# A gated block with segmented attention on one core: the issuing engine of small copies, the place of the late modulation vectors, and the order of the first down-weight scaling

## The chip, the cores and the metric

The kernel runs on one core of one Trainium2 chip. The metric is the device time of one execution in microseconds (us); less is better. The median of three runs before the change is 1928.77 us (1926.87 to 1936.36).

## The reference

x has 2048 rows of 576. From a condition c come six vectors of 576: shift, scale and gate for each of two halves (sa, ca, ga, sb, cb, gb).

```
mod = silu(c) @ w_mod                        # 6 vectors of 576
h   = layernorm(x) * (1 + ca) + sa
x   = x + ga * attention(h)                  # 32 heads of 18, 4 segments of 512 rows
h   = layernorm(x) * (1 + cb) + sb
x   = x + gb * ((silu(h @ w_gate) * (h @ w_up)) @ w_down)   # inner width 4608
```

In the attention each segment s of 512 rows has causal softmax attention within itself, mixed by a sigmoid gate per head with a read from a memory: phi(q) M / phi(q) z, where M and z sum phi(k) v and phi(k) over the earlier segments and phi(t) is t + 1 for t > 0 and exp(t) otherwise. Everything is in float32.

## The kernel before, in words

Products of two float32 matrices are made from a rounded high part and a remainder (hi and lo), so one product is three matmuls. The program has three stages.

**Stage 1, projections (up to about 261 us in the trace).** A loop goes over the four segments s. Within a segment, nine column groups t of q and k are projected (`proj`, matmuls in `mm14` at L99), then four row groups of v (`vproj`, L481 copies the result out). At the end of a segment come the memory sums (`mem`, L433 and L436) and the transposed, scaled input of the next segment (`trans_in`: transposes at L232, ScalarE at L239, and a split into hh on GpSimd, L79, and hl on VectorE, L80). In this stage a scheduler orders each engine's instructions, so that the order on an engine isn't that of the source. Beside the projections run generators, which the loop advances by `next` some times per column or row group:

- `prep(s + 1)` loads and normalises the next segment's rows;
- `late_mod()`, only in segment 1, makes the four vectors that are needed later (p = 2, 4, 3, 5, that is ga, cb, sb, gb). Each is a sum over six blocks k of 96 rows of w_mod: the block is loaded into wml (two buffers) by SyncE, L377, and VectorE multiplies it by one column of silu(c) and adds it to macc (`mod_mul`, L292 for the first and L294 for the others; macc has one buffer). Then TensorE sums macc over its 96 partitions: as a row for all partitions for ga and gb (`mod_row`, L313 into pc, copied to gaB or gbB by ScalarE at L314), as columns for cb and sb (`mod_col`, L301 and L304, L307 and L308). Before the last row group of v, the loop runs out whatever is left of the generators;
- `early()`, from segment 1 on, computes the row maxima of the first attention units.

**Stage 2, attention (about 261 to 656 us).** From here on the order of instructions is written out by hand (`tc.manual_schedule()`). The work is cut into 32 units u of four heads and one segment. A unit has two passes. The first (`p1_step`, matmul L182, VectorE L187) finds each row's maximum of the scores; it is done one or two units ahead. The second (`p2_step`, L579) computes the scores again with the maximum taken off in the same matmul: the stationary kst and the moving qst have 108 rows of data, and rows 108 and 109 of qst hold the negated maxima (hi and lo). ScalarE takes the exponential straight out of PSUM (L582, two PSUM banks s2), GpSimd masks, and TensorE multiplies by v (`av_step`, L599). Between the passes, the maxima of unit u + 1 are transposed (`mt_a`, L201, event m), copied out of PSUM to mr by ScalarE and written into rows 108 and 109 of its qst by two small DMAs (`mt_b`, L205, and `put_m`, L170, event n). One DMA of `put_m` is 16 x 128 numbers, 8 KB. `PAT` is a table that says after which of a unit's eleven steps an event's instructions are issued; event n stands at step 4 of most units, at step 2 of the odd ones in the second half of a segment. SyncE issues nearly all other DMAs of the stage, in program order: the four of `load_stack` for unit u + 3 (L164 and L165), vq, qf (L752), woraw (L884), xr (L676), and stores of xD, xh and yD. An engine that issues a DMA waits in its own order for what the DMA needs.

**Stage 3, feed-forward (about 656 us to the end).** Two halves of the rows t, and in each 18 periods p of two inner blocks, each with 14 steps k of seven matmuls of 512 columns (`prod`, L1180); the down products (L1284, L1301) are worked in a period later. Gate and up weights arrive as O (`load_o`, L1113, two buffers), GpSimd forms four sums of them (`sum_o`, L1135), ScalarE and VectorE split them into wh and wl (`prep_w`, L1144 and L1145). For t = 0 the two rows of blocks of w_down are loaded (`load_d`, L1152), scaled by gbB on GpSimd (`mul_d`, L1158), combined by four differences (`sum_d`, L1163), split for use (`prep_d`, L1169 and L1170), and the whole is stored for t = 1 (L1494). In the first period (`dl` = 2) the steps of `mul_d`, `sum_d` and `prep_d` come two later than in the others: products at steps 6 and 7, differences at 8 to 11, splits at 8 to 11.

The lines of the loop body that set this:

```
if k == 1:
    load_d(0, p)
elif k - dl in (4, 5):
    mul_d(p, k - 4 - dl)
if tn == 0 and 4 <= k < 8:
    sum_o(nx, 0, k - 4)
...
if k - dl in (6, 7, 8, 9) and p < NPR - 2:
    sum_d(p, k - 6 - dl)
```

Of the kernel before, what the change touches and what calls it, by code (L numbers as in the profile page):

```python
# [7 lines left out]
F32 = mybir.dt.float32  # L8
# [9 lines left out]
D = 576  # L18
# [49 lines left out]
def f32(ap):  # L68
    return ap.bitcast(F32)
# [3 lines left out]
def block(ctx: ExitStack, tc: tile.TileContext, x, wqk, wv, wo, beta, wgu, wd, c, w_mod, out):  # L73
    nc = tc.nc
    def pool(stk, name, bufs=1, **kw):
        return stk.enter_context(tc.tile_pool(name=name, bufs=bufs, reuse_waits="tile", **kw))
# [9 lines left out]
    def run(g):  # L86
        for _ in g:
            pass
# [29 lines left out]
    qst, kst = {}, {}  # L118
# [39 lines left out]
    def load_stack(u, b):  # L158
        s, q = units[u]
        for e in range(2):  # L160
            v = [d[s].rearrange("f z t -> (f z) t").rearrange("(Q a e r) t -> Q e r a t", Q=8, a=2, e=2)[q, e]
                 for d in (kD, qD)]
            r = slice(54 * e, 54 * e + 54)
            nc.sync.dma_start(f32(kst[b][r]), v[0])  # L164
            nc.sync.dma_start(f32(qst[b][r, e:4:2, :]), v[1])  # L165

    def put_m(u, b):
        mr = mrow.pop(u)
        for a in range(2):
            nc.scalar.dma_start(f32(qst[b][108 + a:109 + a]).rearrange("p a t -> p (a t)"), mr[16 * a:16 * a + 16])  # L170

    def p1_step(u, b, i, ps, jp, jb):
        if i == 3:
# [34 lines left out]
    def p1_unit(u, b, ps, tag, bufs, jp, jb):  # L208
        for i in range(4):
            yield from p1_step(u, b, 3 - i, ps, jp, jb)  # L210
        mt_a(u, ps, tag, bufs)
        mt_b(u)
# [29 lines left out]
    with ExitStack() as p1:  # L242
        wq1 = pool(p1, "wq1")
        raw = pool(p1, "raw1", 2)
# [6 lines left out]
        def early():  # L251
            for u in range(2):
                load_stack(u, u)
            for u in range(NE):
                yield from p1_unit(u, u, ps, "m", 1, pb, 2)
            load_stack(2, 2)
# [26 lines left out]
        wmv = w_mod.rearrange("(k p) (s f) -> s p k f", p=96, s=6)  # L283
# [6 lines left out]
        def mod_mul(a, t, k):  # L290
            if k == 0:
                nc.vector.tensor_scalar(a, t, sg[:, 0:1], None, op0=ALU.mult)  # L292
            else:
                nc.vector.scalar_tensor_tensor(a, t, sg[:, k:k + 1], a, op0=ALU.mult, op1=ALU.add)  # L294
# [22 lines left out]
        with ExitStack() as p0:  # L317
# [41 lines left out]
            for b in range(3):  # L359
                n = P if b < 2 else 64  # L360
# [8 lines left out]
        pk = pb.tile([P, 4, 640], F32, tag="pk", name="pk", bufs=1)  # L369
        nc.gpsimd.memset(pk[:, :, 0:64], 0.0)  # L370

        def late_mod():
            for p in (2, 4, 3, 5):
                a = raw.tile([96, D], F32, tag="macc", name="macc", bufs=1)
                for k in range(6):
                    t = raw.tile([96, D], F32, tag="wml", name="wml", bufs=2)
                    nc.sync.dma_start(t, wmv[p][:, k, :])  # L377
                    mod_mul(a, t, k)
                    if k % 2:
                        yield  # L380
                if p == 2:
                    mod_row(a, gaB)
                elif p == 4:
                    mod_col(a, 0, 1.0)
                elif p == 3:
                    mod_col(a, 1, 0.0)
                else:
                    mod_row(a, gbB)
                yield

        hT = {}

        def trans_in(s):
            hh = [h1.tile([P, L], F32R, tag=f"hh{k}", name=f"hh{k}") for k in range(4)]
            hl = [h1.tile([P, L], F32R, tag=f"hl{k}", name=f"hl{k}") for k in range(4)]
            hr = h1.tile([P, L], F32R, tag="hr", name="hr")
            hT[s] = (hh, hl, hr)
            for kt in range(5):
                pt = ps.tile([P, L], F32, tag="t", name="pt")
                transpose_group(pt, lambda i: xs[s][:, i, :], kt)  # L400
                if kt < 4:
                    evac_split(wk, pt, kt, hh[kt], hl[kt], colv[:, kt, 0:1], colv[:, kt, 1:2])
                else:
                    evac_split(wk, pt, kt, hr, None, colv[:, kt, 0:1], colv[:, kt, 1:2])
                yield
# [92 lines left out]
        for s in range(NSEG):  # L498
            gens = []
            if s == 0:  # L500
                gens.append(load_wv())
            if s + 1 < NSEG:
                gens.append(prep(s + 1))
            if s == 1:
                gens.append(late_mod())
            g = chain(*gens)
            if s == 1:
                for b in range(3):
                    new_stack(b, sk)
                ge = early()  # L510
            pend = None
            for t in QKORD:
                if s == 0 and t + 4 < 9:
                    load_qk(t + 4)
                f = proj(s, t)
                if pend is not None:
                    phi_k(s, *pend)
                    pend = None
                if t < 5 and s < 3:
                    pend = (t, f)  # L520
                if s > 0 or t > 1:
                    next(g, None)
                    next(g, None)
                if s > 0:
                    for _ in range(E1):
                        next(ge, None)
            tg = trans_in(s + 1) if s + 1 < NSEG else iter(())
            for i in range(4):
                if i == 3:
                    for _ in g:  # L530
                        pass
                vproj(s, i)
                next(g, None)
                next(g, None)
                if s > 0:
                    for _ in range(E2):
                        next(ge, None)
                if i == 2:
                    next(tg, None)
            next(tg, None)  # L540
            if s < 3:
                for _ in mem(s):
                    next(tg, None)
            for _ in tg:
                pass
        run(ge)

    p2, p2r = ExitStack(), ExitStack()
    sk2 = pool(p2, "sk2")
# [345 lines left out]
    NPR = NF // 2  # L895
# [260 lines left out]
    def mul_d(p, f):  # L1156
        v = RW[p][:, 2 * f:2 * f + 2].rearrange("p a b -> p (a b)")
        nc.gpsimd.tensor_tensor(v, v, gbB, op=ALU.mult)  # L1158

    def sum_d(p, j):  # L1160
        r = RW[p]
        d, a, b = ((4, 1, 0), (5, 3, 4), (6, 2, 5), (1, 3, 1))[j]
        nc.gpsimd.tensor_tensor(r[:, d], r[:, a], r[:, b], op=ALU.subtract)  # L1163
# [156 lines left out]
    with tc.manual_schedule():  # L1320
# [5 lines left out]
        for u in range(NU + 1):  # L1326
            s, q = divmod(u, 8)
# [48 lines left out]
        for i in range(4):  # L1376
            for h in range(2):
                for c in range(WC):
                    n = 8 * i + 4 * h + c
# [4 lines left out]
                    if n in SS:  # L1384
                        j = SS.index(n)
# [3 lines left out]
                    if n in WW:  # L1389
                        j = WW.index(n)  # L1390
# [20 lines left out]
        n, nw = 0, PF  # L1411
# [5 lines left out]
        for t in range(2):  # L1417
            for p in range(NPR):
                last = t == 1 and p == NPR - 1
                dl = 2 if t == 0 and p == 0 else 0  # L1420
# [14 lines left out]
                for k in range(14):  # L1435
# [23 lines left out]
                    if t:  # L1459
                        if k == 2 + swap:  # L1460
                            prep_r(1, p, 1)
                        elif not last and k == 9:
                            prep_r(1, nx, 0)
                    else:
                        if k in (3, 5):
                            prep_r(0, p, 1, k // 5)
                        elif tn == 0 and k in (9, 10):
                            prep_r(0, nx, 0, k - 9)
                        elif tn and k == 8:
                            prep_r(1, 0, 0)  # L1470
                        if k == 1:
                            load_d(0, p)
                        elif k - dl in (4, 5):
                            mul_d(p, k - 4 - dl)
                        if tn == 0 and 4 <= k < 8:
                            sum_o(nx, 0, k - 4)
                        elif tn == 0 and k in (10, 11):
                            sum_o(nx, 1, 2 * k - 20)
                            sum_o(nx, 1, 2 * k - 19)
                        if k - dl in (6, 7, 8, 9) and p < NPR - 2:  # L1480
                            sum_d(p, k - 6 - dl)
                        if k == 0 and p == 0:
                            store_o(p, 0)
                            store_o(p, 1)
                        elif k == 3:
                            store_r(p, 0)
                        elif k == 8:
                            store_r(p, 1)
                        elif k == 11 and tn == 0:
                            store_o(nx, 0)  # L1490
                        elif k == 13 and tn == 0:
                            store_o(nx, 1)
                        if k == 12 + dl // 2:
                            nc.scalar.dma_start(wdD[p][:, :NS[p]], RW[p][:, :NS[p]])  # L1494
# [28 lines left out]
                    if is_plain(t, p):  # L1523
                        if k in DK[dl // 2]:
                            j = DK[dl // 2].index(k)
# [74 lines left out]
```

## Time and profile before

| | |
|---|---|
| Median of three runs | 1928.77 us |
| Profiled execution, its own time | 1926.03 us |
| Span of that execution, first to last instruction | 1924.3 us |
| Granted TensorE clock over the span, mean | 0.996 |
| DMA moved | 301.82 MB, 157 GB/s |
| SyncE's hardware queue (q1) | 242.27 MB |
| ScalarE's hardware queue (q10) | 57.60 MB |

Times in the profile are microseconds from the first instruction, unless ns is given. Engines are PE (TensorE matmuls), PEld (its weight loads), DVE (VectorE), ACT (ScalarE), POOL (GpSimd), SP (SyncE); a q behind the name is the engine's sequencer, which issues DMAs. L12 is line 12 of the kernel. In a row of the time order stand the start, the duration, the engine, the line, the operation and tiles (out <- in), how many were merged, and in brackets how long the engine was idle before and what ended that. A row of waits reads: who waited, for whom, us in total, times, longest. A row of the chain of waits has start, duration and name; the chain is followed back from the last instruction, at each step to what released it. A row of a group ends with busy time, mean ns of one, and the idle time before them.

### The profile page before, as it was taken

How to read it: one execution, taken by the hardware profiler on the slowest of the kernel's cores; microseconds unless marked ns; L12 is line 12 of the kernel's file. 1: busy time of each engine (PE TensorE's matmuls, PEld its weight loads, DVE VectorE, ACT ScalarE, POOL GpSimd, SP SyncE). 2: the span in 40 equal slices, each digit the busy share in tenths (PEclk: the TensorE clock that was granted, in tenths of full speed). 3: DMA queues.
4: the chain of work that ended last, by engine and by line, in shares of the span. 5: the costliest groups of instructions: out<-in, count | busy, mean ns of one | idle time of the engine just before them, and what ended most of it. 6: DMA issues, size and time to landing. Idle time of an engine off the chain costs nothing.

```text
span 1924.3 us, 30666 instructions
## 1 busy us (share of the span) xinstructions
PE 1879.5 (98%) x10927; PEld 1561.4 (81%) x10927; DVE 1505.2 (78%) x3270; ACT 930.7 (48%) x2057; POOL 584.3 (30%) x787
## 2 busy tenths in 40 slices
PE   7999999999999999999999999999999999999999
PEld 4887865676666778888888888888888888888888
DVE  6575258777786688898897988876888888888887
ACT  1222257767767544445445445444544444454542
POOL 5212235455546453545444544410000000000000
PEclk9999999999999999999999999999999999999999
DMA  6776465455743855454454554478333233333331
GB/s 197 259 244 218 166 210 138 121 151 144 195 137 112 274 185 184 150 187 158 160 182 153 168 169 144 138 244 269 101 111 108 80 122 101 122 101 96 105 108 61
DMA packets 177856, 301.82 MB, mean 157 GB/s; under 512 B 26024, under 2 KB 106344, under 8 KB 175912
## 3 DMA queue, kind: packets, MB, share of 16 engines
q1 hardware_dynamic: 147080, 242.27, 40.7%
q10 hardware_dynamic: 30624, 57.60, 8.5%
q8 instruction: 86, 1.41, 0.3%
q14 instruction: 66, 0.54, 0.1%
HBM read 186.73 MB, written 112.53 MB: 156 GB/s over the span
## 4 chain that ended last, share of the span: by engine, by line
PE 89%; DVE 3%; DMA 3%; ACT 2%; issue 1%; ACTq 1%; POOL 1%; SPq 0%; DVEq 0%; POOLq 0%
PE A L1180 23%; PE pd L1301 13%; PE C L1180 12%; PE pd L1284 9%; PE B L1180 6%; PE pp L99 5%; PE s L579 4%; PE av L599 3%; PE s L182 3%; PE pv L99 3%; PE pw L709 2%; ACT Pt L582 1%; ACTq L170 1%; PE pn L780 1%; PE pm L433 1%
## 5 line engine op out<-in xcount | busy, mean ns | idle before, releaser
L1180 PE MATMUL A<-y,wh 128*128 128x512 f32 x1152 | 406.6, 393 | 1.9 <-ACT tc L1209 1.0
L187 DVE CUSTOM_DVE_ANT_0 junk<-s,tri 128x256 bf16<-128x256 f32 (+3 forms) x512 | 229.1, 487 | 78.8 <-PE s L182 71.3
L1145 DVE TENSOR_TENSOR wl<-O,wh 128x256 fp32r<-128x256 f32 x504 | 259.4, 520 | 2.5 <-ACT wh L1144 2.0
L1180 PEld LDWEIGHTS A<-y,wh 128*128 128x128 f32 x1152 | 217.0, 188 | 46.5 <-ACT tc L1209 1.8
L582 ACT ACTIVATE Pt<-s 128x512 f32<-128x512 f32 (+1 forms) x352 | 185.5, 559 | 88.0 <-PE s L579 49.5
L1180 PE MATMUL A<-y,wl 128*128 128x512 f32 x576 | 227.0, 394 | 0.0
L1135 POOL TENSOR_TENSOR O<-O 128x384 f32<-128x384 f32 x144 | 163.8, 1149 | 180.5 <-DMA O<-in_wgu_dram 85.8
L1289 DVE TENSOR_TENSOR acc<-acc,pd 128x576 f32<-128x576 f32 x216 | 162.5, 752 | 58.7 <-PE pd L1284 51.5
L1180 PE MATMUL C<-y,wh 128*128 128x512 f32 x576 | 203.1, 393 | 3.8 <-DVE cu L1203 3.8
L1144 ACT CAST wh<-O 128x256 fp32r<-128x256 f32 x504 | 196.8, 405 | 0.8 <-issue 0.8
L1301 PE MATMUL pd<-dh,ah 128*128 128x288 f32 x640 | 189.1, 295 | 0.0
L1301 PE MATMUL pd<-dh,al 128*128 128x288 f32 x640 | 189.1, 295 | 0.0
L1301 PE MATMUL pd<-dl,ah 128*128 128x288 f32 x640 | 188.9, 295 | 0.0
L1305 DVE TENSOR_TENSOR acc<-acc,pd 128x576 f32<-128x576 f32 x156 | 116.9, 750 | 85.3 <-PE pd L1301 84.7
L579 PE MATMUL s<-qs,ks 110*128 110x512 f32 (+2 forms) x384 | 151.7, 411 | 10.9 <-ACT Pt L582 8.9
L1244 ACT CAST ah<-sg 128x512 fp32r<-128x512 f32 x192 | 119.1, 621 | 84.6 <-DVE sg L1204 84.4
L1245 DVE TENSOR_TENSOR al<-sg,ah 128x512 fp32r<-128x512 f32 x192 | 137.1, 714 | 10.8 <-ACT ah L1244 10.6
L182 PE MATMUL s<-ks,qs 108*128 108x256 f32 (+3 forms) x512 | 140.1, 326 | 1.4 <-DVE mx L187 1.4
L1284 PE MATMUL pd<-dh,ah 128*128 128x288 f32 x448 | 133.0, 297 | 0.0
L1284 PE MATMUL pd<-dh,al 128*128 128x288 f32 x448 | 132.5, 296 | 0.0
L1284 PE MATMUL pd<-dl,ah 128*128 128x288 f32 x448 | 132.3, 295 | 0.0
L1180 PEld LDWEIGHTS C<-y,wh 128*128 128x128 f32 x576 | 108.4, 188 | 24.5 <-DVE cu L1203 4.2
(357 smaller groups left out, 4407.8 us busy)
## 6 DMA issues: line engine op xcount, KB each, us to landing
O<-in_wgu_dram SPq DMA_DIRECT2D x36, 768.0 KB
oD<-O ACTq DMA_DIRECT2D x36, 512.0 KB
O<-oD SPq DMA_DIRECT2D x36, 512.0 KB
ks<-kD SPq DMA_DIRECT2D x64, 216.0 KB
qs<-qD SPq DMA_DIRECT2D x64, 216.0 KB
O<-in_wgu_dram SPq DMA_DIRECT2D x36, 384.0 KB
rD<-wr ACTq DMA_DIRECT2D x36, 336.0 KB
wr<-rD SPq DMA_DIRECT2D x35, 336.0 KB
```

Source lines behind the costliest of these rows:

```text
L99: nc.tensor.matmul(ps, lhsT=a, rhs=b, start=(k == 0), stop=(k == 13))
L182: nc.tensor.matmul(bank[:, n * (h - h0):n * (h - h0) + n], lhsT=qst[b][0:108, h, 128 * i:128 * i + 128], rhs=kst[b][0:108, h // 2, 0:n], s ...
L187: nc.vector.tensor_tensor_reduce(junk[:, :n], bank[:, n * (h - h0):n * (h - h0) + n], tri[:, L - n:], 1.0, -3e38, op0=ALU.add, op1=ALU.max ...
L579: nc.tensor.matmul(bank[:, n * (g - h):n * (g - h + w)].rearrange("p (a b) -> p a b", a=w), lhsT=kst[u % NB][0:110, g // 2, 128 * j:128 * ...
L582: nc.scalar.activation(pt[:, h:h + per, :n], bank[:, :n * per].rearrange("p (a b) -> p a b", a=per), AF.Exp, scale=SCALE)
L1135: nc.gpsimd.tensor_tensor(o[:, d], o[:, a], o[:, b], op=op)
L1144: nc.scalar.copy(wh, o)
L1145: later.append(lambda: nc.vector.tensor_tensor(wl, o, f32(wh), op=ALU.subtract))
L1180: nc.tensor.matmul(bank, lhsT=a, rhs=b, start=(first and n == 0), stop=(n == 6), skip_group_check=not first)
L1284: nc.tensor.matmul(pd[:, i, :288], lhsT=a[:, tk], rhs=w, start=(k == 0), stop=(k == 2))
L1289: nc.vector.tensor_tensor(o, o, pd[:, :, :288], op=ALU.add)
L1301: nc.tensor.matmul(pd[:, i, :288], lhsT=a[:, tk], rhs=w, start=(k == 0), stop=(k == 5))
```

## The change

Three edits stand in one diff.

- **A.** The two DMAs of `put_m` are issued by SyncE in place of ScalarE: 64 in all, 60 of them in stage 2.
- **B.** `late_mod` leaves the chain of generators of segment 1. It becomes a generator of its own, made in segment 1 and advanced once after each of the last three row groups of v there, and once after each column and row group in segments 2 and 3. It yields once per block and once more per vector. A block's load is issued one step ahead of its `mod_mul`.
- **C.** In the first feed-forward period only, the down weights are loaded in step 0 (before: step 1), both products and the first three differences are issued in step 2 (before: steps 6, 7, 8, 9 and 10), the fourth in step 11 as before. Thereby they stand ahead of the `sum_o` instructions of steps 4 to 7 in GpSimd's order.

In the instruction order that comes out, SyncE's DMAs from stage 2 on are those of before with the 60 copies put in: in a unit they stand behind the loads of unit u + 3 and ahead of the qf, woraw or xr loads. The instruction order on GpSimd in the first period is two products, three differences, four sums of O, two sums, the fourth difference, two sums. On VectorE, the four accumulations that finish ga stand between the hl instructions ahead of segment 2, and the six of sb among those ahead of segment 3; the pc matmuls of gb come behind the last matmul of segment 3.

```diff
     def put_m(u, b):
         mr = mrow.pop(u)
         for a in range(2):
-            nc.scalar.dma_start(f32(qst[b][108 + a:109 + a]).rearrange("p a t -> p (a t)"), mr[16 * a:16 * a + 16])
+            nc.sync.dma_start(f32(qst[b][108 + a:109 + a]).rearrange("p a t -> p (a t)"), mr[16 * a:16 * a + 16])
...
+        def load_ml(p, k):
+            t = raw.tile([96, D], F32, tag="wml", name="wml", bufs=2)
+            nc.sync.dma_start(t, wmv[p][:, k, :])
+            return t
+
         def late_mod():
-            for p in (2, 4, 3, 5):
-                a = raw.tile([96, D], F32, tag="macc", name="macc", bufs=1)
-                for k in range(6):
-                    t = raw.tile([96, D], F32, tag="wml", name="wml", bufs=2)
-                    nc.sync.dma_start(t, wmv[p][:, k, :])
-                    mod_mul(a, t, k)
-                    if k % 2:
-                        yield
+            pk_ = [(p, k) for p in (2, 4, 3, 5) for k in range(6)]
+            t = load_ml(*pk_[0])
+            for n, (p, k) in enumerate(pk_):
+                nt = load_ml(*pk_[n + 1]) if n < 23 else None
+                yield
+                if k == 0:
+                    a = raw.tile([96, D], F32, tag="macc", name="macc", bufs=1)
+                mod_mul(a, t, k)
+                t = nt
+                if k < 5:
+                    continue
+                yield
                 if p == 2:
                     mod_row(a, gaB)
...
                     mod_row(a, gbB)
-                yield
...
-            if s == 1:
-                gens.append(late_mod())
             g = chain(*gens)
             if s == 1:
...
                 ge = early()
+                gl = late_mod()
...
+                if s > 1:
+                    next(gl, None)
...
                     for _ in range(E2):
                         next(ge, None)
+                    if s > 1 or i > 0:
+                        next(gl, None)
...
         run(ge)
+        run(gl)
...
-                        if k == 1:
+                        if k == 1 - dl // 2:
                             load_d(0, p)
-                        elif k - dl in (4, 5):
-                            mul_d(p, k - 4 - dl)
+                        elif dl and k == 2:
+                            mul_d(p, 0)
+                            mul_d(p, 1)
+                            for j in range(3):
+                                sum_d(p, j)
+                        elif dl and k == 11:
+                            sum_d(p, 3)
+                        elif not dl and k in (4, 5):
+                            mul_d(p, k - 4)
...
-                        if k - dl in (6, 7, 8, 9) and p < NPR - 2:
-                            sum_d(p, k - 6 - dl)
+                        if not dl and k in (6, 7, 8, 9) and p < NPR - 2:
+                            sum_d(p, k - 6)
```

## The prediction, made before the changed kernel was run

> **What bounds the kernel now.** I read the page first, then the busy time by stage.
>
> ```profile
> span 1924.3 us, 30666 instructions
> PE 1879.5 (98%) x10927; PEld 1561.4 (81%) x10927; DVE 1505.2 (78%) x3270; ACT 930.7 (48%) x2057; POOL 584.3 (30%) x787
> ```
>
> TensorE is busy 98% of the span and no other engine is near it, so an edit can pay only where TensorE stands still or runs at a lower clock. The stretches of the three edits show how much of that there is. The columns are: length, busy time and instructions of each engine, granted clock, DMA share, GB/s.
>
> ```profile
> 96.00:131.00 35.00, 34.03 (x181) 27.48 (x180) 31.90 (x91) 7.35 (x15) 7.12 (x11) 1.00 0.77 246
> 148.00:160.00 12.00, 7.82 (x27) 5.18 (x26) 5.16 (x7) 2.19 (x5) 2.35 (x3) 0.72 0.43 163
> 170.00:219.00 49.00, 48.78 (x294) 42.91 (x293) 17.79 (x32) 13.91 (x25) 11.16 (x18) 1.00 0.49 180
> 208.00:220.00 12.00, 11.54 (x77) 9.86 (x76) 5.13 (x10) 3.39 (x5) 4.66 (x9) 1.00 0.26 108
> 261.00:640.00 379.00, 366.05 (x2646) 244.31 (x2645) 289.44 (x1179) 269.07 (x556) 204.51 (x387) 1.00 0.53 147
> 656.00:692.00 36.00, 30.28 (x120) 23.07 (x119) 29.71 (x46) 21.34 (x48) 16.41 (x14) 0.95 0.74 249
> 730.00:1924.00 1194.00, 1190.03 (x6512) 1046.94 (x6510) 1002.01 (x1673) 554.85 (x1285) 259.93 (x234) 1.00 0.44 140
> ```
>
> After 730 us there is nothing to win (4.0 us idle in 1194), and none of the edits acts there. What can be won lies in three places: the end of segment 1 (148 to 160: 4.2 us idle and a clock of 0.72), the attention stage (261 to 640: 13.0 us idle), and the first feed-forward period (656 to 692: 5.7 us idle and a clock of 0.95).
>
> **Edit B, modulation vectors over two segments.** The waits of TensorE from 131 to 170 us, then of VectorE from 96 to 170, then the group of the accumulations, then rows of TensorE and ScalarE in order of time, and one of the chain:
>
> ```profile
> PE pc L313 <- DVE macc L294: 2.5, 1, 2.5
> PE pp L99 <- DVE hl L80: 1.7, 1, 1.7
> DVE macc L294 <- DMA wml<-in_w_mod_dram: 9.9, 7, 2.3
> L294 DVE SCALAR_TENSOR_TENSOR macc<-wml,sg,macc 96x576 f32<-96x576 f32 x20 | 16.5, 823 | 10.0 <-DMA wml<-in_w_mod_dram 9.9
> 155.50 1.33 PE L313 MATMUL pc<-macc,ones 96*128 96x288 f32 x2 [2.50 <-DVE macc L294]
> 114.26 0.75 PE L313 MATMUL pc<-macc,ones 96*128 96x288 f32 x2
> 156.87 0.40 ACT L314 COPY gbB<-pc 128x288 f32<-128x288 f32 x1 [7.79 <-PE pc L313]
> 193.08 11.20 PE pv L99 x84
> ```
>
> Before, all 24 rows of weights go through segment 1, each loaded when it is to be used. VectorE stands 9.9 us for these loads, and what is behind it in its order (hl, the low half of the next segment's input) stands with it. TensorE, in order too, stands at pc. The same two matmuls take 1.33 us at 155 us and 0.75 at 114, since the clock has fallen after the gap.
> The sum: 148 to 160 has 12.00 - 7.82 = 4.2 us of idle. At a mean clock of 0.72, 12 x 0.28 = 3.4 us of clock are missing, which is 6.7 us at half speed; 2.5 of them are the wait of pc, the other 4.2 are work at half speed, 2.1 us lost. That is 6.3 us. The next boundary, without the vectors (208 to 220), runs 77 matmuls at 11.54 busy, so the loss isn't the boundary's own. I add 1.5 us for the first part of segment 1 (96 to 131), where VectorE is busy 31.90 of 35 us and loses the 0.82 us accumulations; this is an estimate between 0 and the 4 us that five of them take.
> Against it: the 24 accumulations move mostly to segments 2 and 3. There VectorE works 17.79 of 49 us, so some 10 us more is hidden. But in the changed kernel's order four of them stand between the hl instructions of the 1-to-2 boundary and six at the 2-to-3 boundary, with two buffers, so that every third load waits for an accumulation: I charge 0.5 us. And the last vector, gbB, is now broadcast after the last matmul of segment 3 and ahead of the attention stage, bare where it had company: half of 0.75, 0.40 for its copy out of PSUM, and the second half's 0.75, 1.5 us. SyncE's loads of the first unit stand behind the last wml loads, but are due only when the stage begins.
> Net of B: 6.3 + 1.5 - 0.5 - 1.5 = **5.8 us won**, bounds 2 and 8.
>
> **Edit A, copies of the row maxima by SyncE.** Waits of TensorE and of its weight loads in 261 to 640, the chain's shares there, a case, and SyncE's queue just before it:
>
> ```profile
> PE s L579 <- ACT Pt L582: 8.9, 22, 1.0
> PE s L579 <- DMA qs<-mr: 1.3, 1, 1.3
> by line: PE s L579 20.1%; PE av L599 17.4%; PE s L182 14.9%; PE pw L709 9.4%; ACT Pt L582 6.5%; ACTq L170 4.7%; PE pn L780 3.7%; issue 2.9%; PE px L620 1.9%; DMA qs<-qD 1.8%; DMA qs<-mr 1.7%; PE pt L946 1.5%; PE pto L682 1.5%; PE pmt L201 1
> ```
> ```profile
> 334.26 0.27 SPq L164 DMA_DIRECT2D ks<-kD  x1
> 335.35 0.34 SPq L165 DMA_DIRECT2D qs<-qD  x1
> 335.74 0.47 SPq L752 DMA_DIRECT2D qf<-qF  x1
> 338.63 0.24 ACT L205 COPY mr<-pmt 32x128 f32<-32x128 f32 x1
> 338.90 1.15 ACTq L170 DMA_DIRECT2D qs<-mr  x2
> 340.10 0.98 ACT L582 ACTIVATE Pt<-s 128x512 f32<-128x512 f32 x2 [1.23 <-PE s L182]
> 340.75 0.44 PE L579 MATMUL s<-qs,ks 110*128 110x384 f32 x1 [0.30 <-ACT Pt L582]
> ```
>
> In each unit ScalarE issues two copies for 1.15 us, with an exponential ready behind them; TensorE then waits for the bank. The chain puts 4.7% of 379 us = 17.8 us on the issue, but that is not the gain: here TensorE was idle for 0.30 us only. The whole of such waits is 8.9 us, the longest 1.0, shorter than one issue; so a wait behind an issue can go whole. Of ScalarE's 11.2% in the chain the issue has 4.7, so 3.7 of the 8.9 us; TensorE's first matmul after a wait also pays a refill that no row prices singly. I take **4.5 us won**, bounds 0 and 10.2 (8.9 + 1.3).
> On SyncE the copy waits for mr. By the changed order, behind it stand the qf, woraw and xr loads: qf of 335.74 would now go after 338.90, some 4 us later with both issues (0.35 each by the rows above), and is read in the next unit. The loads ahead (ks, qs of unit u+3) have gone 3 us before mr is ready. In a few late units SyncE itself is a little behind; the copy has the rest of its unit, 379/32 = 11.8 us, to land.
>
> ```profile
> 296.54 6.58 DMA qs<-mr
> ```
>
> This is the worst of the chain: it cost the 1.3 us above. *DMA: Bandwidth & Descriptors* of the Trainium skill, section "Queues, rings and completion order", says that each DMA engine takes packets in turn from the rings of SP and of ACT, and goes through one ring in order; so the move would take from the copy its turns and set it behind all earlier loads (rival 2). The trace only half agrees: with a ring of its own this copy still took 6.58 us, about as long as the loads ahead of it.
>
> **Edit C, first period's down weights.** SyncE, GpSimd, ScalarE, VectorE and TensorE in order of time:
>
> ```profile
> 656.66 0.83 SPq L1152 DMA_DIRECT2D dr__8790<-in_wd_dram  x2
> 662.09 0.41 DVE L1145 TENSOR_TENSOR wl<-O,wh 128x256 fp32r<-128x256 f32 x1
> 662.43 5.85 DMA O<-in_wgu_dram
> 668.41 2.41 POOL L1135 TENSOR_TENSOR O<-O 128x384 f32<-128x384 f32 x2 [16.45 <-DMA O<-in_wgu_dram]
> 670.78 1.42 POOL L1158 TENSOR_TENSOR dr__8790<-dr__8790,gbB 128x576 f32<-128x576 f32 x1
> 672.24 0.43 ACT L1169 CAST dh<-dr__8790 128x288 fp32r<-128x288 f32 x1 [2.70 <-POOL dr__8790 L1158]
> 673.42 1.65 DVE L1145 TENSOR_TENSOR wl<-O,wh 128x256 fp32r<-128x256 f32 x1
> 685.07 0.50 PE L1180 MATMUL C<-y,wh 128*128 128x512 f32 x1 [3.80 <-DVE cu L1203]
> L1163 POOL TENSOR_TENSOR dr__8790<-dr__8790 128x288 f32<-128x288 f32 x4 | 4.3, 1064 | 0.1
> L1158 POOL TENSOR_TENSOR dr__8790<-dr__8790,gbB 128x576 f32<-128x576 f32 x2 | 3.1, 1532 | 0.0
> ```
>
> GpSimd idles 16.45 us for O, then does the sums of O and the scaling mixed until the stage's end; ScalarE waits 2.70 us for a scaled half, and VectorE, whose wl takes 1.65 us beside GpSimd and 0.41 without, runs late until TensorE stands 3.80 us for cu. Moved ahead of O, two products and three differences (3.1 + 3 x 1.06 = 6.3 us) fall into the idle 16.45 us: the loads go at 656.66 as before (an xD store ahead sets that, not step 1 or 0); if they take the 5.85 us of O, the work ends at 662.5 + 6.3 = 668.8, 0.4 us past O's landing. After it GpSimd is 6.3 us emptier. ScalarE's 2.70 us go, and most of the 3.80: I take **3.5 us won** of the 36.00 - 30.28 = 5.7 us idle and the 36 x 0.05 = 1.8 us of clock. Bounds: -2 (wl slows by up to 1.2 us, twice, between 662 and 668) and 7.
> *SBUF — State Buffer* of the Trainium skill, section "SBUF: two separate sides", says that GpSimd and a VectorE instruction with two SBUF inputs exclude each other for a whole instruction; by it the 6.3 us hold VectorE up wherever they stand, and C would win nothing if VectorE had no slack before 668 us. The 1.65 against 0.41 us agree with the exclusion.
>
> **The sum** against the profiled execution's 1926.0 us (its span and 1.7 around it): 5.8 + 4.5 + 3.5 = 13.8, so 1912.2. The median of the three runs, 1928.77, lies 2.7 above that execution; for a median I add not quite 1: **1913.0 us**. About 0.5%, 9.6 us, is what a measurement of this kernel tells from no change.
>
> **Rivals.**
> 1. *Only B pays* (chance 0.20): TensorE is at 96.6% from 261 to 640 and another releaser ends each wait (weight loads wait beside it), and C's exclusion eats its gain. 1926.0 - 5.8 + 1 = 1921. For: 0.30 us of idle behind 1.15 us of issue. Against: the waits on Pt, 8.9 us.
> 2. *Late copies* (0.09): in SyncE's ring each copy stands behind the loads of unit u+3 and lands after its unit has begun, which decides as soon as the ring is more than about 7 us behind when mr is ready. At 2 us a unit, 30 units: 60 us slower, 1926.0 - 9.4 + 60 = 1977. Against: one wait of 1.3 us in all now, and the loads go 3 us before.
> 3. *The spread accumulations hold the boundaries* (0.13): the loads' round trip moves with them, and hl at 1-to-2 waits as before. B's 5.8 become 0: 1926.0 - 8.0 + 1 = 1919. For: the order. Against: the matmuls of v ahead leave time for two loads to land (the 11.20 us above are three quarters of a segment's).
> That the copies, loads or products stay where they were is excluded: the orders of SP, DVE and POOL show them moved.
>
> **Chances.** Forecast 0.58 (own range 1903 to 1918), rivals 0.20, 0.09, 0.13. Faster by over 0.5% (below 1919.1): 0.55 of the forecast, 0.05 each of rivals 1 and 3: 0.65. Within 0.5%: 0.03 + 0.15 + 0.08 = 0.26. Slower: 0.09. The range: all upper bounds, 25 us, give 1902; the upper end is 1927 with rivals 1 and 3 inside and rival 2 outside.
>
> **What would show it.** B: no wait of pc on macc over 1 us, clock 1.00 between 131 and 170, span to the attention stage shorter by about 6 us. A: no ACTq L170 in the chain, waits of s on Pt nearer 5 than 9 us, no new wait on DMA qs<-mr. C: no wait of dh on POOL, cu's 3.80 under 1.5, clock near 1.00. Wrong if s waits for qs<-mr in most units, or hl at a boundary waits behind macc.

## The result and the profile after

The changed kernel takes 1910.34 us in the median of four runs (1908.17 to 1914.23); before, on the same chip, 1929.21 us. The ratio is 0.9898, with a 95% interval from 0.9866 to 0.9931: faster by 19.7 us, or 13.3 to 25.9. A second session of five runs gave 1912.87 us and 0.9919 (0.9905 to 0.9934). The forecast was 1913.0 us. The total is right; how it comes about is not, as the stages show, so part of the agreement is luck. The profiled execution took 1914.23 us, the slowest of the first four; its page:

```profile
span 1912.5 us, 30679 instructions
PE 1873.4 (98%) x10927; PEld 1560.1 (82%) x10927; DVE 1508.3 (79%) x3270; ACT 934.6 (49%) x2057; POOL 589.5 (31%) x787
```

The busy time by stage, in the columns that the prediction explains, with the stretches moved by what had been won up to there:

```profile
96.00:131.00 35.00, 33.46 (x172) 26.72 (x171) 25.99 (x85) 7.07 (x14) 7.51 (x14) 1.00 0.65 214
148.00:160.00 12.00, 11.21 (x60) 8.96 (x60) 10.80 (x26) 3.36 (x5) 6.62 (x10) 1.00 0.67 226
206.00:216.00 10.00, 7.35 (x39) 5.70 (x40) 5.67 (x9) 2.03 (x3) 4.81 (x7) 1.00 0.23 69
260.00:629.00 369.00, 362.47 (x2649) 246.15 (x2648) 288.87 (x1179) 272.19 (x555) 205.52 (x387) 0.99 0.54 151
644.60:680.60 36.00, 30.00 (x124) 22.50 (x123) 32.09 (x46) 22.07 (x49) 17.45 (x14) 1.00 0.72 242
718.00:1912.00 1194.00, 1190.28 (x6514) 1047.43 (x6512) 1002.97 (x1673) 554.68 (x1285) 259.51 (x234) 1.00 0.44 141
```

The hole of segment 1 (148 to 160) is filled: 11.21 of 12 us busy at full clock, against 7.82 at 0.72. A new one is at the next boundary (206 to 216: 2.65 us idle). In attention the idle time went from 13.0 to 6.5 us, in a stretch 10 us shorter. In the first feed-forward period TensorE still stands 6.0 of 36 us. The long rest is as it was.

To compare kernels, three durations are read from each trace: **segments**, from the first projection matmul to the first score matmul of unit 0; **attention**, from there to the first score matmul of unit 31; **period 1**, the first 98 feed-forward products. What follows period 1, up to the last matmul, takes 1235 to 1237 us in every trace, and the stretch between the last two durations 33 to 34.

| kernel | median, us | ratio (95%) | segments | attention | period 1 |
|---|---|---|---|---|---|
| before | 1929.21 | | 232.4 | 362.0 | 29.6 |
| changed | 1910.34 | 0.9898 (0.9866 to 0.9931) | 231.7 | 351.7 | 29.1 |
| 1 A alone | 1916.26 | 0.9927 (0.9911 to 0.9943) | 238.7 | 351.6 | 29.6 |
| 2 B alone | 1926.10 | 0.9983 (0.9974 to 0.9991) | 232.4 | 364.0 | 29.6 |
| 3 C alone | 1927.98 | 0.9992 (0.9983 to 1.0002) | 234.7 | 364.4 | 28.5 |
| 4 vectors off the boundary | 1910.38 | 0.9893 (0.9877 to 0.9908) | 228.9 | 348.4 | 28.6 |
| 5 one copy each | 1914.34 | 0.9924 (0.9912 to 0.9936) | 232.3 | 350.4 | 29.0 |
| 6 ScalarE filled | 1919.74 | 0.9964 (0.9951 to 0.9978) | 233.3 | 356.6 | 28.8 |
| 7 copies ahead of loads | 1991.45 | 1.0323 (1.0309 to 1.0337) | 233.3 | 428.4 | 29.2 |
| 8 no scaling | 1908.89 | 0.9900 (0.9887 to 0.9914) | 232.1 | 348.0 | 26.4 |
| 9 changed, again | 1912.87 | 0.9919 (0.9905 to 0.9934) | 233.4 | 348.0 | 28.7 |
| 10 as 4, again | 1907.71 | 0.9896 (0.9879 to 0.9913) | 228.9 | 350.3 | 29.2 |
| 11 as 4, vq behind | 1906.08 | 0.9889 (0.9871 to 0.9907) | 227.3 | 348.6 | 29.2 |
| 12 ScalarE doubled | 1966.16 | 1.0196 (1.0178 to 1.0213) | 232.4 | 402.5 | 29.1 |

Each ratio is to runs of the kernel before in the same session; experiments 1 to 4, 5 to 8 and 9 to 12 were run together. One duration comes from one trace, so rows with the same code in a stage show how much it varies: attention from 362.0 to 364.4 us with both copies on ScalarE (before, 2, 3) and from 348.0 to 351.7 with both on SyncE and nothing else changed in the stage (changed, 1, 4, 8, 9, 10). The second spread lies in units 3 and 4, which take from 20.7 to 25.0 us there, where a copy can come late (see 11): the other 29 units take 326.7 to 327.7 us in these six traces and in 11, and 339.0 to 341.6 in the three with both copies on ScalarE.

### The profile page after: what moved, and what is told of

It is laid out like the page before. It is cut to its first block, busy times and chain, and to the rows that moved or that the text cites. A ratio compares the mean times of both kernels' runs of the same rounds, so it can differ in the third digit from the quotient of the medians.

```text
span 1912.5 us, 30679 instructions
## 1 busy us (share of the span) xinstructions
PE 1873.4 (98%) x10927; PEld 1560.1 (82%) x10927; DVE 1508.3 (79%) x3270; ACT 934.6 (49%) x2057; POOL 589.5 (31%) x787
## 4 chain that ended last, share of the span: by engine, by line
PE 91%; DVE 3%; DMA 2%; ACT 1%; POOL 1%; issue 1%; SPq 0%; ACTq 0%; DVEq 0%; POOLq 0%
PE A L1192 23%; PE pd L1313 13%; PE C L1192 12%; PE pd L1296 9%; PE B L1192 6%; PE pp L99 6%; PE s L591 4%; PE av L611 4%; PE s L182 4%; PE pv L99 3%; PE pw L721 2%; PE pn L792 1%; PE px L632 1%; PE pr L350 1%; DVE wl L1157 1%
```

## The experiments

**1 to 3. Each edit alone.** The edits are the three parts of the diff, each put on the kernel before.

> Edit A alone on the kernel before. Theory T1 (from the two traces: the attention stage, first unit to first unit of the last, took 362.0 us before and 351.7 with all three edits): edit A carries nearly the whole result, 10 us here, so about 1919 us against 1929, and the stage at 352 us. Rival R1 (the sum of the prediction): edit A is worth 4.5 us, the stage takes about 357.5 us and the whole about 1924.5; the rest of the stage's gain came from B or C, or from chance.

> Edit B alone. T1: TensorE no longer stands at pc in segment 1 (some 7 us won up to segment 2), but VectorE stands behind a late wml at the 2-to-3 boundary and the last two pc matmuls stand bare ahead of the attention stage, so the first attention unit begins only about 1 us earlier than before (259.5 against 260.5) and the whole is within 2 us of before. R1: 5.8 us won, first unit at about 254.7, the whole about 1923.

> Edit C alone. T1: from the first feed-forward matmul to that of the second period it takes 29.1 us as with all edits, against 29.6 before, so 0.5 us won: GpSimd's work has moved but VectorE, which it holds up, stays the engine that is late; cu's wait falls from 3.8 to about 1.7 us and waits on copies of ScalarE come up. R1: 3.5 us won, 26 us for the period, the whole about 1925.5.

Of 1929.32 us, A alone wins 14.1 (11.0 to 17.2), B alone 3.3 (1.7 to 5.0), C alone 1.5 (-0.4 to 3.3). Together that is 18.9, so the edits do not disturb each other in a way that could be measured. T1 is right that A carries the result, and even too low for it. For B, T1 compared one trace with one trace and came out too low: the kernel before needs 232.4 us for the segments in its own trace, but 238.7 and 234.7 with the same code there in experiments 1 and 3, a mean of 235.3. Eight traces with B as in the diff (the changed kernel, 2, 5 to 9, 12) lie between 231.7 and 233.4, mean 232.6. So B is worth 2.7 us by stages, which fits its 3.3 by time. For C, the interval leaves out R1's 3.5 us and not T1's 0.5, and cu's wait is 1.7 us as T1 said.

**4 and 10. The late vectors away from the boundary.**

```diff
                 if s > 1:
                     next(gl, None)
+                    next(gl, None)
...
-                    if s > 1 or i > 0:
-                        next(gl, None)
```

> All three edits, but the generator of the late vectors is advanced twice after each column group of segments 2 and 3 and not after row groups, so that fewer accumulations stand in VectorE's order at the 2-to-3 boundary and the pc matmuls of gbB come inside segment 3. T1 (accumulations waiting for wml among mbd and hl at that boundary, and the bare pc matmuls at the end, gave back what segment 1 won): the wait of pm on mbd, 2.8 us, falls under 1, gbB's 0.8 and 0.5 us go, the first attention unit begins near 254.5 us in place of 259.5, and the whole is some 5 us below the changed kernel, about 1905. Rival R2 (segments 2 and 3 lost time because 24 loads of wml share the DMA engines with their other transfers, wherever the accumulations stand): the first unit still begins at 258 to 260 us, the whole at 1910.

> The late vectors advanced twice per column group of segments 2 and 3, as in the experiment of that name, beside the changed kernel. In its trace the first unit began 228.8 us after segment 0, against 231.6 to 233.3 in five traces of the changed placement. Theory T1: 3 to 4 us better than the changed kernel, about 1906.5. Rival R2 (the gain of that trace is chance, as the equal medians of 1910.4 and 1910.3 suggest): within 1.5 us of the changed kernel.

The boundary between segments 2 and 3, first in the changed kernel's order of time on VectorE, then on TensorE:

```profile
203.53 0.32 DVE L444 TENSOR_TENSOR mbd<-pm,bdm 128x152 f32<-128x152 f32 x1 [0.67 <-PE pm L441]
206.81 0.81 DVE L294 SCALAR_TENSOR_TENSOR macc<-wml,sg,macc 96x576 f32<-96x576 f32 x1 [2.97 <-DMA wml<-in_w_mod_dram]
207.55 0.30 DVE L444 TENSOR_TENSOR mbd<-pm,bdm 128x152 f32<-128x152 f32 x1
```
```profile
207.91 0.53 PE L441 MATMUL pm<-vs,pk 128*128 128x152 f32 x2 [1.98 <-DVE mbd L444]
```

An accumulation waits 2.97 us for its block of weights; the mbd behind it waits too, and TensorE, which has one bank for pm, stands 1.98 us. The same stretch, 204 to 218 us, in the changed kernel run again and in experiment 10:

```profile
204.00:218.00 14.00, 11.99 (x62) 10.27 (x62) 6.16 (x11) 2.28 (x4) 6.15 (x10) 0.88 0.37 121
```
```profile
204.00:218.00 14.00, 13.50 (x89) 11.30 (x89) 5.67 (x14) 2.93 (x5) 6.06 (x10) 1.00 0.34 130
```

With the accumulations out of the way TensorE does 89 matmuls where it did 62, at full clock. In both traces of this placement the segments take 228.9 us, nearly 4 less than the mean of the changed placement. The edit moves two things, and the traces price them apart. From the start of segment 2's last pv matmul to that of segment 3's it takes 54.7 us in 4 and 10, 56.4 in the changed kernel and 56.5 in its second trace: 1.8 us for the accumulations at the boundary. And the pc matmuls of gb, which stood bare ahead of the attention stage, now stand inside segment 3: the first score matmul starts 0.1 us after the start of the last pv, against 2.8, which is 2.7 us. T1 is right in both; the first unit begins at 256.4 and 256.3 us, between its 254.5 and R2's 258, because segment 0, which no edit touches, took 54.2 us in these two traces and 52.6 in that of the changed kernel. The times are less sharp: experiment 4 came out level with the first median of the changed kernel, experiment 10 is 5.2 us below the changed kernel beside it, with intervals that overlap. So the gain of about 4 us and its two parts are shown by the traces; the times only fit them.

**5. One copy on each engine.**

```diff
-            nc.sync.dma_start(f32(qst[b][108 + a:109 + a])...
+            (nc.sync if a else nc.scalar).dma_start(f32(qst[b][108 + a:109 + a])...
```

> All three edits, but of the two copies of each unit the first is issued by ScalarE again and the second by SyncE. In the traces edit A took the stage from first unit to last unit's begin from 362 to 364 us down to 348 to 352, some 12 us for 64 issues. Theory T2 (every issue holds up ScalarE by its 0.57 us and the stage pays it in proportion): half of it comes back, the stage takes about 357 us, the whole about 1916. Rival R3 (only a delay longer than the slack of the two score banks reaches TensorE; 0.57 us is hidden and 1.15 is not): the stage stays within 2 us of 351, the whole about 1911.

Attention takes 350.4 us, inside the range without any issue on ScalarE, so R3 is right that half of the issues doesn't bring half of the cost back. Without units 3 and 4 it takes 329.1 us, 1.4 to 2.4 above the seven traces with both copies on SyncE, and the median, 1914.34, lies 1.5 to 4 us above those of the changed kernel: it costs about 2 us, where half would be 7.

**6. ScalarE filled, the DMAs left on SyncE.**

```diff
         put_m(u, u % NB)
+        if u >= NE:
+            for _ in range(2):
+                du = mwk.tile([P, L], BF16, tag="du", name="du", bufs=1)
+                nc.scalar.copy(du, tri)
```

> All three edits, and behind the copy to mr ScalarE makes two additional copies of 128 x 512 numbers to a tile that nobody reads, about 1.1 us as the two issues had taken; the DMAs stay on SyncE. T2 (the gain of edit A is ScalarE's time ahead of a ready exponential): the stage is back at about 362 us, the whole at about 1922. Rival R4 (the gain comes from the copies' way through the other queue, for instance rows 108 and 109 landing earlier): the stage stays at about 351 us, the whole at 1910.

**12. The same, with the copies issued by ScalarE as before.** The diff is that of experiment 6 and edit A undone.

> Edits B and C, the two copies issued by ScalarE as before, and behind them the two additional copies of 128 x 512 numbers on ScalarE that nobody reads, so that a unit holds up ScalarE by about 2.2 us. So far: 0.57 us per unit cost nothing in the trace of the stage (350.4 us), 1.07 us 6 us, 1.15 us of issue some 12 us. Theory T6 (a delay up to about 0.7 us is taken up by the two score banks, and beyond it each microsecond of ScalarE costs a microsecond per unit): 31 units x 1.07 us on top of 363 us, the stage at about 396 us, the whole at 1958. Rival R7 (ScalarE is busy under three quarters of the stage and catches up within the unit, so the cost stays in proportion to what the first 1.15 us cost): the stage at about 375 us, the whole at 1936.

The attention stage of both, from unit 0 to unit 31, ahead of them the kernel before and the changed kernel:

```profile
260.50:622.50 362.00, 350.17 (x2516) 232.46 (x2514) 282.74 (x1163) 259.07 (x537) 194.26 (x374) 1.00 0.52 143
```
```profile
259.50:611.20 351.70, 346.26 (x2514) 234.14 (x2514) 282.33 (x1163) 262.06 (x536) 194.94 (x374) 0.99 0.53 148
```
```profile
260.50:617.10 356.60, 348.66 (x2515) 232.38 (x2515) 282.64 (x1163) 289.94 (x596) 194.30 (x374) 1.00 0.53 146
```
```profile
260.20:662.70 402.50, 366.90 (x2514) 240.21 (x2514) 283.89 (x1163) 292.36 (x596) 195.71 (x374) 0.96 0.48 130
```

One pair of copies in experiment 6:

```profile
349.31 0.25 ACT L205 COPY mr<-pmt 32x128 f32<-32x128 f32 x1
349.46 1.26 ACT L210 CAST du<-tri 128x512 bf16<-128x512 f32 x2
350.63 0.86 ACT L598 ACTIVATE Pt<-s 128x384 f32<-128x384 f32 x2
```

They take 1.26 us, a little more than the 1.15 of the two issues, but they hold ScalarE up for less: the first begins 0.10 us before the copy to mr ends, and the next exponential 0.09 before the second ends, where the issues overlap neither. From the end of that copy to the start of ScalarE's next exponential it takes 1.07 us here and 1.23 in the rows of the prediction (338.87 to 340.10). As a median over the 30 units whose copies fall into this stretch, up to ScalarE's next instruction that is no copy to du, that time is 0.12 us in the changed kernel, 0.60 in experiment 5, 1.07 in 6, 1.23 before and 2.40 in 12. The pairs bring attention from about 349.5 us (mean of the seven traces with both copies on SyncE and ScalarE not filled: changed, 1, 4, 8 to 11) to 356.6, which is 7.1 us; the two issues bring it to 363.4 (mean of 362.0, 364.0 and 364.4), which is 13.9. So ScalarE's time is the cause, as T2 says, but not in proportion, and R4, which expected no change with the DMAs left on SyncE, is out. On top of the issues the same pair costs 402.5 - 363.4 = 39.1 us, about 30 units x 1.26 = 37.8: beyond a certain delay every microsecond of ScalarE is about a microsecond of each unit, as T6 says, and R7 (375 us) is out. Per unit the stage pays 0.24 us for the delay of 1.07, 0.46 for 1.23 and 1.77 for 2.40, so 0.6 to 0.8 us of delay are not paid. That the pair of copies costs half of what the issues cost is then for the most part its shorter delay: 0.16 us in 30 units are 4.8 of the 6.8 us between them, and one trace each doesn't tell the rest from chance.

**7. The copies ahead of the loads.**

```diff
-            load_unit(u + 3)
-            if 3 <= q < 7 and s < 3:
-                load_v(s + 1, q - 3)
...
                     event(ev, u)
+                    if ev == "n":
+                        load_unit(u + 3)
+                        if 3 <= q < 7 and s < 3:
+                            load_v(s + 1, q - 3)
```

> All three edits, and in each unit the loads for unit u + 3 are issued behind the two copies of row maxima in place of ahead of them. Theory T3 (in SyncE's queue the copy for unit 4 stands behind some 1 MB of loads and takes 7.1 us, which costs a wait of 2.7 us and work at half clock after it): the copy lands in about 2 us, the wait on it goes, 3 us won, about 1907. Rival R5 (the DMA engines are busy, in whatever order; in the kernel before that copy took 6.6 us in a queue of its own): the copy takes 6 us or more still, and the loads, some 5 us later, are waited for in other units: 1911 to 1920.

Slower by 3.2%. In the trace, TensorE's largest wait from 258 to 645 us and SyncE's own from 260 to 690:

```profile
PE s L182 <- DMA ks<-kD: 32.7, 18, 3.1
```
```profile
SPq L170 <- ACT mr L205: 143.5, 19, 12.0
```

SyncE stands at the copy until ScalarE has written mr, and the 864 KB of loads behind it stand with it. TensorE has no wait for a copy left in the stage, as T3 expected, but its waits for loads cost far more. R5 is right in its second half, at some 80 us over the changed kernel where at most 10 were expected. The changed kernel has the same wait, shorter,

```profile
SPq L170 <- ACT mr L205: 54.0, 15, 6.0
```

and what stands behind the copy there (qf, woraw, xr) is due later.

**11. The load of vq behind the copies**, on top of experiment 10.

```diff
-            if 3 <= q < 7 and s < 3:
-                load_v(s + 1, q - 3)
...
                     event(ev, u)
+                    if ev == "n" and 3 <= q < 7 and s < 3:
+                        load_v(s + 1, q - 3)
```

> As the one before, and the load of vq for the next segment (312 KB, in the units 3 to 6 of a segment) is issued behind the copies of row maxima in place of ahead of them; it is needed only a segment later. Theory T5 (a copy's landing time is the load that stands ahead of it in the queue): the copy for unit 4 lands a microsecond sooner, its wait falls from 2.7 or 1.6 us to under 1, and the whole is 1 to 2 us better than with the load ahead. Rival R5 (the DMA engines are busy with other loads all the same): no difference over 0.5 us.

TensorE's waits for copies from 285 to 320 us, where the one for unit 4 lands: in the changed kernel, in experiment 10 and in 11:

```profile
PE s L591 <- DMA qs<-mr: 2.7, 1, 2.7
```
```profile
PE s L590 <- DMA qs<-mr: 2.1, 1, 2.1
```
```profile
PE s L590 <- DMA qs<-mr: 0.8, 1, 0.8
```

For unit 4 the second trace of the changed kernel has 1.1 us and experiment 4 has 0.9. The wait is not all that a late copy costs: units 3 and 4 take 25.0 us in the changed kernel and 20.9 in its second trace, and the granted clock from 300 to 306 us is 0.50 in the first and 1.00 in the second. In experiment 11 the copy for unit 4 is out of the chain of waits, and the 0.8 us are for the one of unit 5, issued in the next unit, which still needs 6.19 us:

```profile
293.31 7.10 DMA qs<-mr
```
```profile
297.48 6.19 DMA qs<-mr
```

The first is the changed kernel's for unit 4, the second experiment 11's for unit 5. So T5 holds for the unit that it spoke of; a slow copy is not cured by it, as R5 says. The median of 1906.08 us is the lowest of all kernels here, 0.9889 of the kernel before (0.9871 to 0.9907), but 1.6 us below experiment 10 is less than these runs tell apart.

**8. No scaling in the first period.**

```diff
                         elif dl and k == 2:
-                            mul_d(p, 0)
-                            mul_d(p, 1)
-                            for j in range(3):
-                                sum_d(p, j)
-                        elif dl and k == 11:
-                            sum_d(p, 3)
+                            nc.gpsimd.memset(RW[p][:, 4:7], 0.0)
```

> All three edits, with the scaling and the four differences of the first period's down weights left out (three blocks are set to zero by one memset in their place), so that the down products of that period are not the reference's. Theory T4 (edit C won little because GpSimd's 7.6 us of this work hold VectorE up wherever they stand: between 649 and 656 us its wl, y and wr instructions take about 3 us longer than the same ones elsewhere): the first period takes about 26 us from 29.1, the whole about 1907. Rival R6 (VectorE is late by its own work and by the sums of O, and the weight work is already hidden): within 0.7 us of the changed kernel.

First GpSimd and VectorE in the changed kernel:

```profile
649.03 3.48 POOL L1170 TENSOR_TENSOR dr__8782<-dr__8782,gbB 128x576 f32<-128x576 f32 x2 [8.31 <-DMA dr__8782<-in_wd_dram]
```
```profile
649.41 1.81 DVE L1038 TENSOR_TENSOR y<-yh,y 32x512 fp32r<-32x512 f32 x1
...
652.72 1.29 DVE L1036 TENSOR_TENSOR y<-yh,y 128x512 fp32r<-128x512 f32 x1
654.04 1.04 DVE L1142 TENSOR_TENSOR wr<-O,wr 32x384 fp32r<-32x384 f32 x1
```

and the same three instructions of VectorE in experiment 8:

```profile
645.25 0.69 DVE L1038 TENSOR_TENSOR y<-yh,y 32x512 fp32r<-32x512 f32 x1
...
647.04 0.69 DVE L1036 TENSOR_TENSOR y<-yh,y 128x512 fp32r<-128x512 f32 x1
647.76 0.55 DVE L1142 TENSOR_TENSOR wr<-O,wr 32x384 fp32r<-32x384 f32 x1
```

Beside GpSimd's products these three take 4.14 us, without them 1.93. Period 1 takes 26.4 us, 2.5 less than the mean of 28.9 in the ten other traces with C (28.5 to 29.2). T4 is right, R6 out: the work was moved, and it costs where it now stands nearly what it cost before.

## Why the prediction was right in the total and wrong in its terms

The sum was 13.8 us = 5.8 + 4.5 + 3.5; measured by stages it is 17.2 = 2.7 + 13.9 + 0.6 (period 1: mean 29.6 without C in before, 1 and 2, 28.9 with it in ten traces). The mechanisms of A and B are the ones named; all three sizes were off, A too small, B and C too large, and it is luck that they cancel in part.

**A: 4.5 predicted, 13.9 by stages, 14.1 by time, outside the bounds of 0 and 10.2.** The step that failed is "The whole of such waits is 8.9 us", taken as the most that could go, and cut to 3.7 by a share of the chain. The waits did fall, to 1.3 us, and the chain of 260 to 629 us has no ACTq L170 among its lines:

```profile
PE s L591 <- ACT Pt L594: 1.3, 6, 0.5
```

But idle time isn't all that a late bank costs. Two neighbouring matmuls of the changed kernel:

```profile
344.46 0.40 PE L591 MATMUL s<-qs,ks 110*128 110x512 f32 x1
344.70 0.39 PE L182 MATMUL s<-ks,qs 108*128 108x512 f32 x1
```

A matmul of 512 columns counts as busy for 0.40 us, and the next begins 0.24 after its start. A matmul that comes up to 0.16 us late shows no idle time, and one that waits longer shows 0.16 us too little. The weight loads ahead of them show more of these waits; in the whole stage, before and after:

```profile
PEld s L579 <- ACT Pt L582: 50.7, 87, 1.2
```
```profile
PEld s L591 <- ACT Pt L594: 32.4, 58, 0.9
```

Twenty-nine waits fewer, where the matmuls had shown 22 in all. Taken as the time from the start of the matmul before, the 372 score matmuls of units 0 to 30 cost 82.1 us before, 71.7 in the changed kernel and 70.5 in its second trace: 10.4 and 11.7 us, of the 10.3 and 14.0 by which attention is shorter in these two, stand at the one place that was named. Of the 10.3 us between the two windows of the stage above, 6.4 are idle time (11.8 to 5.4) and 3.9 are busy time, for the same work (2516 and 2514 matmuls in the records). The prediction saw the weight loads' waits only as an argument for rival 1.

That one issue per unit costs little (5) and a pair of copies on top of the issues costs its whole length (12) says why a share of the chain was no measure: of ScalarE's delay 0.6 to 0.8 us are taken up between ScalarE and TensorE (1.07 - 7.1 / 30, 1.23 - 13.9 / 30 and 2.40 - 53.0 / 30), and what goes beyond is paid in each unit. These figures are estimates, worked out as if each microsecond beyond cost one.

**B: 5.8 predicted, 2.7 by stages, 3.3 by time.** Its first terms, 7.8 us, held: segments 1 and 2 are 7.6 us shorter in the changed kernel than before, in one trace each and in part because 24 of the 48 pc matmuls now come later; no wait of pc on macc is left between 131 and 170, and the clock is 1.00 there.

```profile
PE pm L441 <- DVE mbd L444: 0.5, 1, 0.5
PE pp L99 <- DVE hr L80: 0.3, 1, 0.3
```

The terms that failed are the two charges. The first is "I charge 0.5 us" for accumulations between the hl instructions. It was seen that six of them stand at the 2-to-3 boundary and that every third load waits for a buffer, but not what one such round trip costs there. In the chain of the changed kernel it begins as an accumulation frees the buffer:

```profile
201.24 5.49 DMA wml<-in_w_mod_dram
```

That is 2.97 us of VectorE and 1.98 of TensorE, and in three of the eight traces with this placement (6, 7 and 9) a clock of 0.88 from 204 to 218 us, against 1.00 in the others. Taking the accumulations away from there won 1.8 us (4 and 10). It was rival 3's mechanism, at the other boundary than the one that the rival named. The second is the bare pc of gbB, charged at 1.5 us. It cost 2.7, since its second half waits for the first to be copied out:

```profile
258.29 0.75 PE L313 MATMUL pc<-macc,ones 96*128 96x288 f32 x2 [0.80 <-ACT gbB L314]
259.53 0.50 PE L591 MATMUL s<-qs,ks 110*128 110x512 f32 x1 [0.49 <-ACT gbB L314]
```

From the end of the last pv (257.0) to the first score matmul are 2.5 us; in 4 and 10 the score matmul starts 0.2 us ahead of that end. With 1.8 and 2.7 us in place of 0.5 and 1.5, the sum for B is 3.3.

**C: 3.5 predicted, 0.6 by stages, 1.5 by time (-0.4 to 3.3).** What was to go went: no wait of dh on GpSimd, cu's 3.80 us are 1.7 (not quite under 1.5), the clock is 1.00. What came in their place are waits on ScalarE and VectorE, from 644 to 682:

```profile
PE A L1192 <- ACT tb L1221: 1.8, 1, 1.8
PE C L1192 <- DVE cu L1215: 1.7, 1, 1.7
PE A L1192 <- ACT B L1238: 1.0, 1, 1.0
```

The step that failed is "fall into the idle 16.45 us": idle on GpSimd, but not free, because VectorE had no slack there. VectorE is busy 32.09 of 36 us, more than before (29.71). The rule of the Trainium skill that the prediction set against this (*SBUF — State Buffer*, "SBUF: two separate sides", GpSimd and a VectorE instruction with two SBUF inputs exclude each other) agrees with the trace: 4.14 against 1.93 us for the three instructions. The lower bound had priced that exclusion; the value taken had not.

**The rivals.** Rival 1 is right for C and wrong for A, so its 1921 us did not come. Rival 2 did not come: one copy was late, for 2.7 us, and such copies in SyncE's queue took from 5.2 (experiment 1) to 7.1 us there, about the 6.58 that it took in a queue of its own. That the loads go ahead of the copy was what kept it away from the other danger, the loads being late (7).

## What to carry to other kernels

Idle time of TensorE was a lower bound of what a late producer cost here, not an upper one: matmul rows overlap, so read the starts, or the waits of the weight loads, before you cap a gain. A small DMA issued by an engine that feeds TensorE costs little while its delay is shorter than what the buffers between the two take up, and its full excess in every unit beyond that; move it to an engine that doesn't feed TensorE, behind the loads that are due early there. Work moved into one engine's idle time is only free if the engine that it blocks is idle too, and a chain of loads with two buffers should not cross a stage's boundary on an engine on which the boundary waits.

## What was not expected of the hardware

- Two issues of 0.57 us on ScalarE cost attention 13.9 us, two copies, 1.26 us in the same place, 7.1. Read from the end of the copy ahead of them, the issues held ScalarE up for 1.23 us and the longer copies for 1.07, because the copies overlap what stands ahead of them and behind them by about 0.1 us each.
- In the changed kernel SyncE waited 15 times for mr, up to 6.0 us, and TensorE waited for no load by it; with the loads behind that wait instead of ahead of it (7), attention took 428.4 us and the granted clock fell to 0.92.
- The same segment code took 232.4, 234.7 and 238.7 us in three traces; with the late vectors spread over two segments it stayed within 1.7 us in eight.
